# Banded attention in 24-query tiles on the quarters of the partitions, with one softmax per job, before two gated layers on one core

## The chip, the cores and the metric

The kernel runs on one core of one Trainium2 chip. The metric is the device time in microseconds (us) of one execution. Three runs of the kernel before gave 1005.63, 1005.64 and 1008.18 us; the median is 1005.64 us.

## The reference

Inputs are q, k, v of 4 batches x 8 heads x 576 positions x 64, and weights of two gated layers. In float32:

```python
q_d, k_d, v_d = (mean over 4 neighbouring positions of q, k, v)     # 144 positions
out_up    = repeat(softmax(q_d @ k_d.T / 8) @ v_d, 4)               # down-sampled attention
out_local = softmax(where(|i - j| < 4, q @ k.T / 8, -1e9)) @ v      # banded attention
x  = (out_up + out_local) as 2304 tokens x 512
y  = (sigmoid(x @ w_gate) * (x @ w_val)) @ w_out                    # 512 -> 1536 -> 512
h  = y @ w_in;  out = (h * sigmoid(1.702 h)) @ w_out2               # 512 -> 2048 -> 512
```

## The kernel before, in words

**Jobs.** Attention is cut into 16 jobs, one per batch and pair of heads (class Job, L409); head 0 of a pair lies on partitions 0 to 63, head 1 on 64 to 127. A job loads q and k, transposed (L433, L434), loads v grouped by fours for the down-sampled part (vg, two DMAs, L436) and v in five overlapping pieces of at most 122 rows for the band (vt, five DMAs, L444). Its steps are:

- pools (L466): GpSimd adds neighbours of q and k (L450, L452); VectorE sums v over four (L472).
- scores (L475): the band in five units of 116 queries by 122 keys, each in two parts of 64 and 52 queries against 70 and 58 keys, two heads: 20 products (L487), which the trace shows as 40 matmuls, since each fp32 product is two.
- soft (L495): per unit and part, one VectorE instruction adds the mask, scales and finds the extreme (L501), ScalarE takes the exponential with a sum (L508); the sums are inverted (L512, L513) and GpSimd multiplies (L519).
- the transpose of the probabilities: for batch 0 on TensorE with copies by ScalarE (full_transpose, L550, L555), for the other batches as 14 VectorE transposes of 32-row blocks (L535).
- down, soft_d, down_t (L559 to L625): the down-sampled attention, 144 by 144, with its products (L568), extremes (L584), exponentials (L591), sums (L595, L596), GpSimd multiplication (L604) and TensorE transposes (L618).
- values and combine (L627, L661): products with v (L644, L650), then VectorE adds the two parts (L667) and the sum is split into a high and a low part for the layers (L672, L674).

**Layers.** The tokens go through layer 1 in five visits (one per batch, the last for the four tails of 64 tokens together), then through layer 2 in five. Each product of the layers is three matmuls of 512 columns (passes, L744 to L749: high times high, low times high, high times low). The first visit, that of batch 0, has 12 blocks of 36 such matmuls, 432 in all. Layer 1's weights come as 64-bit words and are made into float32 by VectorE and ScalarE in the first visit (bits and signed: L696, L698, L700, L705), 36 pieces of 512 KB; splitting them into high and low takes ScalarE and GpSimd (L711, L713). VectorE also makes the gated product of each block (L783, L787).

**Order.** Class Plan (L62) orders all instructions at build time. Each has an assumed cost and a due time; on each engine the earliest due among the ready ones comes first, and SyncE's queue (SP) of DMAs is ordered in the same way, with an assumed rate (L73) and time per issue (L193). The due times follow from T0, the assumed start of the layers (L381), and EARLY (L384). Weights are asked for no earlier than 15 us ahead of their due time (AHEAD, L386), which is 8 us ahead of the block that uses them. Where TensorE would stand idle before the first layer products, it is given small filler matmuls on zeros (L917). PSUM has two banks for attention (pa), and while batch 0 is worked four more (acc). At run time each engine goes through its list in this order and waits where an operand is late.

Of the kernel before, what the change touches and what calls it, by code (L numbers as in the profile page):

```python
# [19 lines left out]
P = 128  # L20
# [41 lines left out]
class Plan:  # L62
# [10 lines left out]
    DMA_RATE = 230.0  # L73
# [48 lines left out]
    def order(self):  # L122
# [24 lines left out]
        while count:  # L147
# [44 lines left out]
            if e == "sp":  # L192
                free[e] = t + 60.0  # L193
# [24 lines left out]
def tile_multiscale_attention_gated_ffn(  # L218
# [22 lines left out]
    LW = 128  # L241
# [49 lines left out]
    ring("xf", 2, [P, 348])  # L291
# [10 lines left out]
    qslots, kslots, vslots, pslots, tslots = (plan.rings[nm][0] for nm in ("qt", "kt", "vt", "pt", "tt"))  # L302
# [27 lines left out]
    for s in kslots:  # L330
        nc.gpsimd.memset(s.t[:, :KPAD], 0.0)
        nc.gpsimd.memset(s.t[:, KPAD + S:], 0.0)
    for s in vslots:
        nc.gpsimd.memset(s.t[:32, 0], 0.0)
        nc.gpsimd.memset(s.t[96:, NUN - 1], 0.0)
    masks = [sb.tile([P, n], F32, name=f"mask{i}", tag=f"mask{i}")
             for i, n in enumerate((WIDTH[0], WIDTH[0], WIDTH[1]))]
    nc.gpsimd.memset(masks[1], 0.0)
    for h in range(2):
        half = masks[1][h * D:(h + 1) * D]  # L340
        nc.gpsimd.affine_select(out=half, in_=half, pattern=[[1, WIDTH[0]]], compare_op=ALU.is_ge,
                                fill=NEG, base=0, channel_multiplier=-1)
        nc.gpsimd.affine_select(out=half, in_=half, pattern=[[-1, WIDTH[0]]], compare_op=ALU.is_ge,
                                fill=NEG, base=6, channel_multiplier=1)
# [5 lines left out]
    def unit_mask(u, part):  # L350
        if u == 0 and part == 0:
            return masks[0]
# [604 lines left out]
```

## Time and profile before

| | |
|---|---|
| median of three runs | 1005.64 us |
| the profiled execution's own time | 1005.93 us |
| its span, first to last instruction | 1004.2 us |
| TensorE (PE) busy | 961.4 us, 96% of the span |
| VectorE (DVE) busy | 577.2 us, 57% |
| ScalarE (ACT) busy | 445.3 us, 44% |
| GpSimd (POOL) busy | 322.2 us, 32% |
| mean granted TensorE clock | 0.983 of full speed |
| moved by DMA | 70.96 MB, 71 GB/s over the span |

The busy shares are averages over parts of the run that differ. The span is also shown in 40 slices of 25.1 us, each with the busy share of an engine in tenths, and by windows. In rows of the trace, a name such as pt<-pt,nm says which tile is written and which are read; x56 is a count; "mean ns" is the mean duration of one instruction; the records of neighbouring instructions of one engine overlap a little.

### The profile page before, as it was taken

What the parts mean: (1) busy time and instruction counts of PE and PEld (TensorE: products, weight loads), DVE (VectorE), ACT (ScalarE), POOL (GpSimd) and SP (SyncE); (2) the same over time, 40 slices, a digit from 0 to 9 for tenths busy, and PEclk for the clock granted to TensorE, in tenths of its full rate; (3) what the DMA queues carried; (4) which work ended last, traced back from release to release, by engine and by line L of the source; (5) the groups of instructions that cost most, each with busy time, mean ns of one, the idle gap of its engine ahead of it and who ended that gap; (6) DMA issues with size and microseconds to landing.
All of it is one profiled execution on the core that took longest, in us unless ns stands there. A gap on an engine that the chain in (4) does not pass through costs nothing.

```text
span 1004.2 us, 15460 instructions
## 1 busy us (share of the span) xinstructions
PE 961.4 (96%) x5620; PEld 788.9 (79%) x5620; DVE 577.2 (57%) x1380; ACT 445.3 (44%) x1142; POOL 322.2 (32%) x318
## 2 busy tenths in 40 slices
PE   6889799799999999999999999999999999999997
PEld 5777577688788878888889977788888888888896
DVE  4899999966663576565756689723223222322232
ACT  5755465554544554554556565413223222322222
POOL 5654655544453453353445442102002000100000
PEclk8989899999999999999999999999999999999999
DMA  5664455121111210033204044102001000100010
GB/s 162 185 209 146 140 192 179 31 95 50 51 49 32 72 33 20 24 116 126 85 22 154 16 148 168 42 1 84 1 1 43 32 1 1 52 1 1 1 43 22
DMA packets 45324, 70.96 MB, mean 71 GB/s; under 512 B 5632, under 2 KB 26048, under 8 KB 45248
## 3 DMA queue, kind: packets, MB, share of 16 engines
q1 hardware_dynamic: 45248, 69.97, 21.9%
q8 instruction: 44, 0.72, 0.3%
q14 instruction: 32, 0.26, 0.1%
HBM read 60.00 MB, written 9.96 MB: 70 GB/s over the span
## 4 chain that ended last, share of the span: by engine, by line
PE 72%; DVE 18%; issue 4%; DMA 2%; ACT 2%; POOL 1%; SPq 1%; POOLq 0%; ACTq 0%; DVEq 0%
PE ph L747 13%; PE ph L749 13%; PE ph L748 13%; PE acc L747 10%; PE acc L748 10%; PE acc L749 10%; DVE we L700 3%; DVE we L698 2%; DVE tt L535 2%; DVE w L705 2%; PE pa L487 1%; DVE glo L787 1%; DVE vd L472 1%; DVE we L705 1%; DVE th L783 1%
## 5 line engine op out<-in xcount | busy, mean ns | idle before, releaser
L783 DVE SCALAR_TENSOR_TENSOR th<-th,ph 128x512 f32<-128x512 f32 (+1 forms) x140 | 88.5, 632 | 270.7 <-ACT th L778 212.1
L713 POOL TENSOR_TENSOR wlo<-w,whi 128x512 fp32r<-128x512 f32 x126 | 177.8, 1418 | 172.4 <-ACT whi L711 169.4
L778 ACT ACTIVATE th<-ph 128x512 f32<-128x512 f32 (+1 forms) x140 | 77.4, 553 | 261.6 <-PE ph L749 261.5
L747 PE MATMUL ph<-xhi,whi 128*128 128x512 f32 (+1 forms) x480 | 181.6, 378 | 1.2 <-DVE th L783 1.2
L748 PE MATMUL ph<-xhi,wlo 128*128 128x512 f32 (+1 forms) x480 | 178.0, 371 | 2.2 <-POOL wlo L713 2.2
L749 PE MATMUL ph<-xlo,whi 128*128 128x512 f32 (+1 forms) x480 | 177.7, 370 | 0.0
L711 ACT CAST whi<-w 128x512 fp32r<-128x512 f32 x180 | 110.2, 618 | 108.4 <-PE ph L749 39.2
L787 DVE TENSOR_TENSOR glo<-th,ghi 128x512 fp32r<-128x512 f32 (+1 forms) x140 | 99.3, 709 | 47.7 <-ACT ghi L786 46.6
L747 PE MATMUL ph<-xhi,w 128*128 128x512 f32 (+1 forms) x320 | 119.9, 375 | 1.4 <-DVE th L783 1.3
L749 PE MATMUL ph<-xlo,w 128*128 128x512 f32 (+1 forms) x320 | 119.3, 373 | 0.0
L748 PE MATMUL ph<-xhi,w 128*128 128x512 f32 (+1 forms) x320 | 119.1, 372 | 0.0
L747 PE MATMUL acc<-w,ghi 128*128 128x512 f32 x288 | 114.4, 397 | 1.7 <-ACT ev L826 1.6
L748 PE MATMUL acc<-w,glo 128*128 128x512 f32 x288 | 114.1, 396 | 0.4 <-DVE glo L787 0.4
L749 PE MATMUL acc<-w,ghi 128*128 128x512 f32 x288 | 113.9, 395 | 0.0
L786 ACT CAST ghi<-th 128x512 fp32r<-128x512 f32 (+1 forms) x140 | 80.6, 576 | 63.8 <-DVE th L783 62.6
L747 PEld LDWEIGHTS ph<-xhi,whi 128*128 128x128 f32 x480 | 90.9, 189 | 19.0 <-issue 2.6
L748 PEld LDWEIGHTS ph<-xhi,wlo 128*128 128x128 f32 x480 | 91.0, 190 | 16.7 <-POOL wlo L713 2.6
L749 PEld LDWEIGHTS ph<-xlo,whi 128*128 128x128 f32 x480 | 91.1, 190 | 15.8 <-DVE xlo L674 0.3
L858 POOL TENSOR_TENSOR xlo<-st,xhi 128x512 fp32r<-128x512 f32 (+1 forms) x24 | 30.3, 1275 | 223.3 <-ACT xhi L856 223.2
L747 PE MATMUL acc<-ghi,whi 128*128 128x512 f32 (+1 forms) x240 | 90.5, 377 | 0.0
L748 PE MATMUL acc<-ghi,wlo 128*128 128x512 f32 (+1 forms) x240 | 89.1, 371 | 0.0
L749 PE MATMUL acc<-glo,whi 128*128 128x512 f32 (+1 forms) x240 | 88.9, 371 | 0.0
(104 smaller groups left out, 1470.7 us busy)
## 6 DMA issues: line engine op xcount, KB each, us to landing
w<-w SPq DMA_DIRECT2D x68, 512.0 KB
qt<-qT SPq DMA_DIRECT2D x16, 288.0 KB
kt<-kT SPq DMA_DIRECT2D x16, 288.0 KB
vg<-v SPq DMA_DIRECT2D x32, 144.0 KB
x2d<-ev SPq DMA_DIRECT2D x16, 256.0 KB
st<-x2d SPq DMA_DIRECT2D x16, 256.0 KB
out<-ev SPq DMA_DIRECT2D x16, 256.0 KB
vt<-v SPq DMA_DIRECT2D x48, 61.0 KB
```

The costliest lines, as they stand in the source:

```text
L700: op("dve", 602.0, lambda: nc.vector.scalar_tensor_tensor(e.t, wv[:, :, 0], 29, e.t, op0=ALU.logical_shift_right, op1=ALU.bitwise_or), [w] ...
L705: op("dve", 602.0, lambda: nc.vector.scalar_tensor_tensor(m.t, top, -2 ** 31, e.t, op0=ALU.bitwise_and, op1=ALU.bitwise_or), [w] if m is e ...
L711: op("act", 520.0, lambda: nc.scalar.copy(hi.t, m.t.bitcast(F32)), [m], [hi], due)
L713: op(eng, ns, lambda: on.tensor_sub(lo.t, m.t.bitcast(F32), hi.t.bitcast(F32)), [m, hi], [lo], due)
L747: nc.tensor.matmul(o, lhi, rhi, start=first, stop=False)
L748: nc.tensor.matmul(o, llo, rhi, start=False, stop=False)
L749: nc.tensor.matmul(o, lhi, rlo, start=False, stop=last)
L778: op("act", act_ns(n, True), lambda h=h: nc.scalar.activation(th.t[:, :n], h.t[:, :n], AF.Tanh, scale=0.5 if layer == 1 else 1.702 / 4.0), ...
L783: op("dve", dve_ns(n), lambda: nc.vector.scalar_tensor_tensor(th.t[:, :n], th.t[:, :n], 1.0, hb[-1].t[:, :n], op0=ALU.add, op1=ALU.mult), ...
L786: op("act", act_ns(n), lambda: nc.scalar.copy(gh.t[:, :n], th.t[:, :n]), [th], [gh], t)
L787: op("dve", dve_ns(n), lambda: nc.vector.tensor_sub(gl.t[:, :n], th.t[:, :n], gh.t[:, :n].bitcast(F32)), [th, gh], [gl], t)
L858: op("pool", pool_ns(n), lambda k=k, st=st: nc.gpsimd.tensor_sub(lo.t[:, k, :n], st.t[:, :n], hi.t[:, k, :n].bitcast(F32)), [st, (hi, k)], ...
```

## The change

The band is cut into 24 tiles of 24 queries by 30 keys. Tile NG*i+g (NG = 6) goes to quarter i of the partitions, so that a head's scores are one block of 128 partitions by 6 x 30. Each job then has 48 products of 30 columns for the scores, with tile positions in the array, and one softmax over both heads: VectorE adds the mask (two instructions), takes the maximum, subtracts it, ScalarE takes one exponential over 360 columns, VectorE sums, inverts, multiplies and transposes all 32-row blocks at once. The products with v are 48 of 24 columns, in two halves; the second half is issued after ScalarE has copied out the down-sampled result. The down-sampled softmax takes its maximum with two instructions and its exponentials straight from PSUM. v is loaded, and summed over four, for two jobs at a time. Costs and dates that the plan assumes are altered.

```diff
-    DMA_RATE = 230.0
+    DMA_RATE = 300.0
...
-                free[e] = t + 60.0
+                free[e] = t + 450.0
...
-    NQ, NU = 116, 122
-    WIDTH = (D + 6, NU - D)
-    units = [(0, 0), (116, 0), (232, 0), (348, 0), (460, 4)]
-    NUN = len(units)
+    NQ, NU = 24, 30
+    NT = S // NQ
+    NG = NT // 4
+    VC = 2 * P
+    HALF = S // 2
...
-    for nm, n, shape in (("qt", 2, [P, S + 12]), ("kt", 2, [P, KPAD + S + 5]), ("vt", 2, [P, NUN, P]),
-                         ("pt", 2, [P, NUN, 2, LW]), ("tt", 2, [P, 2 * NUN, LW]), ("vg", 2, [GH, 2, 4, P]),
-                         ("half", 1, [P, G, 2]), ("qd", 2, [P, G]), ("kd", 2, [P, G]), ("vd", 2, [GH, 2, P]),
-                         ("nm", 2, [P, 2, NUN]), ("sm", 2, [P, 2, NUN]), ("pd", 2, [GH, 2, 2, G]),
-                         ("nmd", 2, [GH, 4]), ("smd", 2, [GH, 4]), ("pdt", 1, [GH, 2, 2, G]), ("up", 2, [P, G])):
+    for nm, n, shape in (("qt", 2, [P, S + 12]), ("kt", 2, [P, KPAD + S + 5]), ("vt", 2, [P, NG, VC]),
+                         ("sc", 2, [P, 2, NG, NU]), ("pt", 2, [P, 2, NG, 32]), ("tt", 2, [P, 2, NG, 32]),
+                         ("vg", 1, [GH, 2, 4, VC]), ("half", 1, [P, G, 2]),
+                         ("qd", 2, [P, G]), ("kd", 2, [P, G]), ("vd", 2, [GH, 2, VC]),
+                         ("nm", 2, [P, 2, NG]), ("sm", 2, [P, 2, NG]), ("pd", 2, [GH, 2, 2, G]),
+                         ("nmd", 2, [GH, 4]), ("smd", 2, [GH, 4]), ("pdt", 2, [GH, 2, 2, G]), ("up", 2, [P, G])):
...
+    mask = sb.tile([P, NG, NU], F32, name="mask", tag="mask")
+    band = sb.tile([P, NU], F32, name="band", tag="band")
...
-    QUANTUM = 3 * 216.0
+    QUANTUM = 3 * 227.0
     ATT = 15.0e3
-    T0 = 50.0e3
+    T0 = 37.0e3
...
-    EARLY = 20.0e3
-    FULL_T = 1
+    EARLY = 16.0e3
...
+    class Values:
+
+
+        def __init__(self, m):
+            self.b, self.c0 = m // 2, m % 2 * VC
+            self.job = jobs[2 * m]
+
+        def load(self):
+            b, c = self.b, slice(self.c0, self.c0 + VC)
+            self.vg, self.vt, self.vd = buf("vg"), buf("vt"), buf("vd")
+
+            hp = self.job.hp
+            d, after = (self.job.t0 - 3000.0, self.job.t0 - 12000.0) if b else (4500.0 * hp, 4500.0 * hp)
+            for kh in range(2):
+                dma(self.vg.t[:, kh], v[b, kh * 4 * GH:(kh + 1) * 4 * GH, c].rearrange("(g r) d -> g r d", r=4),
+                    GH * 4 * VC * 4, [], [(self.vg, kh)], d, after)
+            d, after = (self.job.due(0.2), self.job.t0 - 9000.0) if b else (4500.0 * hp + 3000.0, 6000.0 * hp)
+            for i in range(4):
+                g0, g1 = i == 0, NG - (i == 3)
+                row = NQ * (NG * i + g0) - 3
+                src = v[b, row:row + 32, c]
+                src = bass.AP(tensor=src.tensor, offset=src.offset,
+                              ap=[[DM, 32], [NQ * DM, g1 - g0], [1, VC]])
+                dma(self.vt.t[32 * i:32 * i + 32, g0:g1], src, 32 * (g1 - g0) * VC * 4, [], [(self.vt, i)], d, after)
+            dma(self.vt.t[3:NU, 0], v[b, :NU - 3, c], (NU - 3) * VC * 4, [], [(self.vt, 4)], d, after)
+            row = NQ * (NT - 1) - 3
+            dma(self.vt.t[96:96 + S - row, NG - 1], v[b, row:S, c], (S - row) * VC * 4, [], [(self.vt, 5)], d, after)
+
+        def pool(self):
+            vg, vd = self.vg, self.vd
+            at = self.job.due(0.4)
+            op("dve", dve_ns(4 * VC), lambda: nc.vector.tensor_add(
+                vg.t[:, :, :2], vg.t[:, :, :2], vg.t[:, :, 2:]), [], [vg], at)
+            op("dve", dve_ns(2 * VC), lambda: nc.vector.tensor_add(vd.t, vg.t[:, :, 0], vg.t[:, :, 1]),
+               [vg], [vd], at)
...
+            d, after = self.t0 - 4000.0, self.t0 - 13000.0
+            dma(self.qt.t[:, :S], qT[b, hp], P * S * 4, [], [self.qt], d, after)
+            dma(self.kt.t[:, KPAD:KPAD + S], kT[b, hp], P * S * 4, [], [self.kt], d, after)
...
+                for t in range(NT):
+                    g, i = divmod(t, 4)
+                    t = NG * i + g
+                    for h in range(2):
+                        hs = slice(h * D, (h + 1) * D)
+                        nc.tensor.matmul(ss[h].t[32 * i:32 * i + 32, g * NU:(g + 1) * NU],
+                                         qt.t[hs, NQ * t:NQ * t + 32], kt.t[hs, NQ * t:NQ * t + NU],
+                                         start=True, stop=True, tile_position=(h * D, 32 * i))
+
+            n = NG * NU
+            op("pe", 1500.0, pe, [qt, kt], [*ss, (sc, 0), (sc, 1)], self.due(0.1))
+            for h in range(2):
+                op("dve", dve_ns(n), lambda h=h: nc.vector.tensor_add(
+                    sc.t[:, h], ss[h].t[:, :n].rearrange("p (g c) -> p g c", c=NU), mask),
+                   [ss[h]], [(sc, h)], self.due(0.1))
+
+            def spread(x):
+                return x.t[:, :, :, None].to_broadcast([P, 2, NG, NU])
+
+            at = self.due(0.15)
+            op("dve", dve_ns(2 * n), lambda: nc.vector.reduce_max(nm.t, sc.t, axis=AX.X), [sc], [nm], at)
+            op("dve", dve_ns(2 * n), lambda: nc.vector.tensor_sub(sc.t, sc.t, spread(nm)), [nm], [sc], at)
+            p = pt.t[:, :, :, :NU]
+            op("act", act_ns(2 * n), lambda: nc.scalar.activation(p, sc.t, AF.Exp, scale=SCALE), [sc], [pt], at)
+            op("dve", dve_ns(2 * n), lambda: nc.vector.reduce_sum(sm.t, p, axis=AX.X), [pt], [sm], at)
 
             def inv():
+                nc.vector.tensor_scalar_add(sm.t, sm.t, 1.0e-9)
+                nc.vector.reciprocal(sm.t, sm.t)
+
+            op("dve", 305.0, inv, [], [sm], at)
+            op("dve", dve_ns(2 * n), lambda: nc.vector.tensor_mul(p, p, spread(sm)), [sm], [pt], at)
+            op("dve", 700.0, lambda: nc.vector.transpose(
+                out=tt.t.rearrange("p h g c -> p (h g c)"), in_=pt.t.rearrange("p h g c -> p (h g c)")),
+               [pt], [tt], at)
...
+                op("dve", dve_ns(2 * G), lambda h=h: nc.vector.reduce_max(
+                    nmd.t[:, 2 * h:2 * h + 2], ss[h].t[:GH, :2 * G].rearrange("p (r k) -> p r k", k=G), axis=AX.X),
+                   [ss[h]], [(nmd, h)], at)
+            op("dve", 90.0, lambda: nc.vector.tensor_scalar_mul(nmd.t, nmd.t, -SCALE_D), [], [nmd], at)
+
+            def ex(h):
                 for r in range(2):
                     x = 2 * h + r
+                    nc.scalar.activation(pd.t[:, h, r], ss[h].t[:GH, r * G:(r + 1) * G], AF.Exp,
+                                         bias=nmd.t[:, x:x + 1], scale=SCALE_D, accum_out=smd.t[:, x:x + 1])
+
+            for h in range(2):
+                op("act", 1100.0, lambda h=h: ex(h), [nmd, ss[h]], [(pd, h), (smd, h)], at)
...
+            def band(x):
+                for g in range(NG):
+                    for s, i in ((sa, x), (sz, 2 + x)):
+                        ks, q = slice(32 * i, 32 * i + NU), NQ * (NG * x + g)
+                        for h in range(2):
+                            nc.tensor.matmul(s.t[h * D:(h + 1) * D, q:q + NQ],
+                                             vt.t[ks, g, v0 + h * D:v0 + (h + 1) * D], tt.t[ks, h, g, :NQ],
+                                             start=True, stop=True, tile_position=(32 * i, h * D))
 
             def pe():
+                band(0)
                 for kh in range(2):
                     for h in range(2):
+                        nc.tensor.matmul(sa.t[h * D:(h + 1) * D, c0:c0 + G],
+                                         vd.t[:, kh, v0 + h * D:v0 + (h + 1) * D],
                                          pdt.t[:, h, kh, :], start=(kh == 0), stop=(kh == 1))
+
 
             xfs = [buf("xf") for _ in range(2)]
+            op("pe", 1400.0, pe, [vd, pdt, vt, tt], [sa, sz, up, *xfs], self.due(0.9))
+            op("act", 260.0, lambda: nc.scalar.activation(up.t, sa.t[:, c0:c0 + G], AF.Copy, scale=0.25),
                [sa], [up], self.due(0.9))
+            op("pe", 700.0, lambda: band(1), [vt, tt, up], [sa, sz], self.due(0.9))
+            for n, s in enumerate((sa, sz)):
+                self.combine(n * HALF, (n + 1) * HALF, s, xfs[n], n == 0, xh, xl)
...
     jobs = [Job(b, hp) for b in range(B) for hp in range(NHP)]
+    halves = {(m // 2, m % 2): Values(m) for m in range(2 * B)}
     jobs[0].load()
-    jobs[0].load_v()
+    jobs[1].load()
+    halves[0, 0].load()
...
+        if n + 2 < len(jobs):
+            jobs[n + 2].load()
+            if n % 2 == 0:
+                halves[divmod(n // 2 + 1, 2)].load()
```

## Rows read from the trace of the kernel before

**Rows 1.** The page's 40 slices of the span, VectorE.

```profile
DVE  4899999966663576565756689723223222322232
```

**Rows 2.** Windows: length, busy time of PE, PEld, DVE, ACT, POOL, granted clock, DMA.

```profile
0.00:30.00 30.00, 20.24 (x305) 18.43 (x305) 14.63 (x100) 14.37 (x71) 16.09 (x46) 0.83 0.56 162
30.00:66.00 36.00, 28.47 (x380) 24.15 (x379) 34.38 (x110) 23.40 (x104) 22.88 (x28) 0.91 0.64 210
66.00:201.00 135.00, 118.38 (x711) 93.67 (x708) 132.32 (x309) 74.48 (x202) 71.52 (x60) 0.95 0.44 140
201.00:500.00 299.00, 298.82 (x1816) 242.20 (x1815) 189.58 (x558) 159.76 (x452) 136.56 (x129) 1.00 0.20 63
```

**Rows 3.** ScalarE groups, 66 to 201 us: busy, mean ns, idle before and what ended it.

```profile
L711 ACT CAST whi<-w 128x512 fp32r<-128x512 f32 x35 | 21.5, 617 | 34.0 <-DVE w L705 30.9 <-DVE sm L512 1.3 <-DVE smd L595 1.0
```

**Rows 4.** VectorE's busy time to 201 us, lines L501, L535, L472, L584, L512, L513, L527.

```profile
0.00:201.00 201.00, 12.52 (x160) 0.92 0.50 156
0.00:201.00 201.00, 18.79 (x56) 0.92 0.50 156
0.00:201.00 201.00, 17.77 (x9) 0.92 0.50 156
0.00:201.00 201.00, 8.04 (x64) 0.92 0.50 156
0.00:201.00 201.00, 3.07 (x16) 0.92 0.50 156
0.00:201.00 201.00, 3.04 (x16) 0.92 0.50 156
0.00:201.00 201.00, 2.25 (x2) 0.92 0.50 156
```

**Rows 5.** VectorE groups by shape, 201 to 500 us.

```profile
L472 DVE TENSOR_REDUCE vd<-vg 72x256 f32<-72x1024 f32 x7 | 14.0, 2007 | 0.1
...
L667 DVE TENSOR_TENSOR xf<-pa,up 128x348 f32<-128x348 f32 x8 | 4.2, 520 | 12.7 <-ACT up L656 12.5
L674 DVE TENSOR_TENSOR xlo<-xf,xhi 128x348 fp32r<-128x348 f32 x8 | 4.1, 518 | 0.1
...
L667 DVE TENSOR_TENSOR xf<-pa,up 128x228 f32<-128x228 f32 x8 | 3.1, 385 | 0.0
```

**Rows 6.** Timeline of TensorE around two attention blocks: start us, us, what.

```profile
347.24 0.40 PE L748 MATMUL ph<-xhi,wlo 128*128 128x512 f32 x1
347.47 0.40 PE L749 MATMUL ph<-xlo,whi 128*128 128x512 f32 x1
347.80 1.40 PE L487 MATMUL pa<-kt,qt 64*64 64x70 f32 x40
349.13 0.50 PE L747 MATMUL ph<-xhi,whi 128*128 128x512 f32 x1
...
194.22 0.71 PE L644 MATMUL pa<-pdt,vd 72*64 72x144 f32 x8
194.76 1.16 PE L650 MATMUL pa<-tt,vt 122*64 122x116 f32 x20
195.85 0.50 PE L747 MATMUL ph<-xhi,whi 128*128 128x512 f32 x1
```

**Rows 7.** Timeline of TensorE, the last products with v of batch 0.

```profile
63.03 2.13 PE L650 MATMUL acc<-tt,vt 122*64 122x116 f32 x20
```

**Rows 8.** Timeline of SyncE's queue at the start, and the first weight load.

```profile
0.73 0.40 SPq L375 DMA_DIRECT2D qt<-qT  x1
...
1.65 1.86 SPq L375 DMA_DIRECT2D vg<-v  x2
3.55 4.50 SPq L375 DMA_DIRECT2D vt<-v  x5
...
34.51 0.53 SPq L375 DMA_DIRECT2D w<-w  x1
```

**Rows 9.** Timeline of TensorE, two products of different heads.

```profile
30.42 0.34 PE L568 MATMUL pa<-kd,qd 64*72 64x144 f32 x1
30.43 0.34 PE L568 MATMUL acc<-kd,qd 64*72 64x144 f32 x1
```

More of the change, by code (lines that the diff above doesn't have):

```diff
@@ L332, in tile_multiscale_attention_gated_ffn @@
         nc.gpsimd.memset(s.t[:, KPAD + S:], 0.0)
+    mask = sb.tile([P, NG, NU], F32, name="mask", tag="mask")
+    band = sb.tile([P, NU], F32, name="band", tag="band")
+    nc.gpsimd.memset(band, 0.0)
+    for i in range(4):
+        quarter = band[32 * i:32 * i + 32]
+        nc.gpsimd.affine_select(out=quarter, in_=quarter, pattern=[[1, NU]], compare_op=ALU.is_ge,
+                                fill=NEG, base=0, channel_multiplier=-1)
+        nc.gpsimd.affine_select(out=quarter, in_=quarter, pattern=[[-1, NU]], compare_op=ALU.is_ge,
+                                fill=NEG, base=6, channel_multiplier=1)
@@ L333, in tile_multiscale_attention_gated_ffn @@
+    nc.gpsimd.tensor_copy(mask, band[:, None, :].to_broadcast([P, NG, NU]))
+    nc.gpsimd.affine_select(out=mask[:32, 0], in_=mask[:32, 0], pattern=[[1, NU]], compare_op=ALU.is_ge,
+                            fill=NEG, base=-3, channel_multiplier=0)
+    nc.gpsimd.affine_select(out=mask[96:, NG - 1], in_=mask[96:, NG - 1], pattern=[[-1, NU]],
+                            compare_op=ALU.is_ge, fill=NEG, base=S + 2 - NQ * (NT - 1), channel_multiplier=0)
     for s in vslots:
         nc.gpsimd.memset(s.t[:32, 0], 0.0)
-        nc.gpsimd.memset(s.t[96:, NUN - 1], 0.0)
@@ L336, in tile_multiscale_attention_gated_ffn @@
[L336 to L344, printed above, removed]
@@ L345, in tile_multiscale_attention_gated_ffn @@
-    nc.gpsimd.affine_select(out=masks[0], in_=masks[1], pattern=[[1, WIDTH[0]]], compare_op=ALU.is_ge,
-                            fill=NEG, base=-3, channel_multiplier=0)
-    nc.gpsimd.affine_select(out=masks[2], in_=masks[1][:, :WIDTH[1]], pattern=[[-1, WIDTH[1]]],
-                            compare_op=ALU.is_ge, fill=NEG, base=S + 2 - units[-1][0] - D, channel_multiplier=0)
-    def unit_mask(u, part):
-        if u == 0 and part == 0:
-            return masks[0]
-        return masks[2 if u == NUN - 1 and part else 1][:, :WIDTH[part]]
@@ L449, in pool4 @@
             s = src.rearrange("p (g a b) -> p g a b", a=2, b=2)
-            op("pool", 880.0, lambda: nc.gpsimd.tensor_add(half.t, s[:, :, :, 0], s[:, :, :, 1]),
+            op("pool", 760.0, lambda: nc.gpsimd.tensor_add(half.t, s[:, :, :, 0], s[:, :, :, 1]),
                [bsrc], [half], due)
-            op("pool", 520.0, lambda: nc.gpsimd.tensor_add(dst.t, half.t[:, :, 0], half.t[:, :, 1]),
+            op("pool", 450.0, lambda: nc.gpsimd.tensor_add(dst.t, half.t[:, :, 0], half.t[:, :, 1]),
                [half], [dst], due)
         def front(self):
-            steps = [self.pools, self.scores, self.down]
-            if self.first:
-                steps += [lambda h=h, us=us: self.full_transpose(h, us) for h in range(2)
-                          for us in (range(3), range(3, NUN))]
-            return steps
+            return [self.pools, self.scores, self.down]
         def back(self):
@@ L481, in pe @@
             def pe():
-                for part in range(2):
-                    n, c = WIDTH[part], D * part
-                    for u, (q0, _) in enumerate(units):
-                        for h in range(2):
-                            hs = slice(h * D, (h + 1) * D)
-                            nc.tensor.matmul(ss[part].t[hs, u * n:(u + 1) * n], qt.t[hs, q0 + c:q0 + c + D],
-                                             kt.t[hs, q0 + c:q0 + c + n], start=True, stop=True)
-            op("pe", NUN * (56.0 * 2 + 1.667 * sum(WIDTH)), pe, [qt, kt],
-               [*ss, (pt, 0), (nm, 0), (pt, 1), (nm, 1)], self.due(0.1))
@@ L901, in tile_multiscale_attention_gated_ffn @@
                 front[x]()
-                if x == 0 and n + 1 < len(jobs):
-                    jobs[n + 1].load()
             if x < len(back):
```

150 lines of the change are left out of this document (22 added, 128 removed).

## Prediction

> **What bounds the kernel now.** I read the slices first. VectorE is full from the third slice to the eighth and then falls to about two thirds [rows 1]. The windows say what that means. From 201 us on TensorE is busy 298.8 of 299 us, while VectorE is at 189.6 [rows 2]: the rest of the kernel is TensorE's, and only a change in TensorE's own work counts there. From 66 to 201 us it is the other way round: VectorE 132.3 of 135 us, TensorE 118.4, at a granted clock of 0.95 [rows 2]. The weights explain it: ScalarE, which splits them for the first visit, stood idle for 30.9 us until VectorE had made a weight (L705) [rows 3]. So up to 201 us the first visit goes at VectorE's pace, with batch 1's jobs and 36 weights on that engine. Before 66 us batch 0's jobs run; their last products with v come at 63.0 us [rows 7], and no block of the layers can be finished before that. VectorE idles 15.4 of the first 30 us [rows 2]: SyncE needs 4.5 us to issue one job's five vt loads and 1.86 for two of vg, against 0.40 for q [rows 8], and the first weight is not asked for until 34.5 us.
>
> The reading to keep: before 201 us a microsecond off VectorE is worth a microsecond, after it nothing; TensorE's is the reverse.
>
> **VectorE, up to 201 us.** Eight jobs (batches 0 and 1) lie there. The change removes from VectorE L501 12.5 us, L535 18.8, L584 8.0, L512 3.1, L513 3.0, L527 2.2, and of L472 eight of nine instructions, 15.8: 63.4 us in all [rows 4]. What it adds per job, priced by the fit through L667's two shapes (385 ns at 228 columns, 520 at 348, so 128 ns and 1.125 a column) [rows 5]:
> - two additions of the mask, 180 columns: 2 x 0.33 = 0.66;
> - subtraction and multiplication over 360: 2 x 0.53 = 1.06;
> - maximum and sum over 360: no row has a reduction over contiguous columns. L472's strided one took 2007 ns for 1024, 1.96 a column, which gives 0.71 each; the fit gives 0.53. I take 0.53, as the strides are gone, and keep 0.4 to 0.71;
> - inversion, 0.38 (L512 and L513 as now, once instead of twice) [rows 4];
> - the transpose of 384 columns: L535 took 0.336 us for 160 (18.8 over 56) [rows 4], so at most 0.81, and at least 0.43 by the fit's slope; I take 0.7;
> - two maxima over 288 for the down-sampled part, 0.90, and a small product, 0.1;
> - v over four, per two jobs 1024 and 512 columns, 1.28 + 0.70, so 0.99 a job.
>
> That is 5.85 us a job, 46.8 for eight, with bounds of 4.9 and 7.2. The saving is 63.4 - 46.8 = 16.6 us. Records of neighbours overlap a little, so I count 0.93 of it, an estimate: 15.5 us (bounds 22.5 and 5.5).
>
> **The start.** SP's issues per two jobs are now 2 x (0.4 + 0.4) + 2 x 1.86 + 2 x 4.50 = 14.3 us [rows 8]. After: the same 1.6 for q and k, 1.86 for two wider vg loads, and six vt loads at between 0.4 (as q) and 0.9 (as a vt load now), 2.4 to 5.4: at most 8.9 us. Weights may be asked for 13 us earlier, since T0 moves from 50 to 37 us. Both put work before VectorE in the 15.4 idle us. The first 5 us can't be filled; I take 9 of the rest, with 0 and 12 as bounds. GpSimd loses the multiplication L519 and keeps its other work; it has 63 us to spare in the window of 135 [rows 2]. ScalarE loses nine of ten exponentials of the band; it had 60 to spare already, so that is worth nothing by itself. The wider v rows (32 rows per tile of 24 queries) add about a third to vt's bytes; DMA stands at 0.44 busy in the window [rows 2], which covers that. If that cover were gone, the first weights would be late.
>
> **TensorE.** Matmuls come in pairs, one per head, that run side by side. Per pair: L487 1.33 us for 20 pairs of 64 columns on average, 66.5 ns; L650 1.09 for 10 pairs of 115, 109 ns; L644 0.54 for 4 pairs of 144, 135 ns [rows 6]. That is a line: 0.86 ns a column and 12 ns a pair. New scores are 48 pairs of 30 columns at 38 ns, 1.8 us against 1.33. New products with v are 48 pairs of 24 columns at 32.5 ns, 1.55 against 1.09. The second half of them adds one more interruption, 0.1 us (347.47 + 0.23 would be 347.70, and L487 starts at 347.80) [rows 6]. So +1.0 us a job if only pairs overlap. If four tiles overlap, both fall by half: 1.7 - 2.42 + 0.1 = -0.6. The plan's own costs hint at between: 1627 and 1765 ns before, for blocks that take 1.43 and 1.72 on the path [rows 6], become 1500 and 2100, which scaled is +0.2. I take +0.5; the eight jobs of batches 2 and 3 lie where TensorE is the bound, so +4 us. For batch 1 it hides under VectorE: 118.4 + 4 x 0.5 still leaves 14 us. Batch 0's TensorE transposes (L550) go; they lie before the layers and are counted at nothing.
>
> One rule speaks against the change. Rows first: the records of two products of different heads start 10 ns apart [rows 9], so two tiles are not held apart by a long step. The Trainium skill (TensorE: Matmul & The Clock Gate, "Wait — 56ns, not 53.3ns?") says that start-to-start never falls below about 25 ns however small the matmul. By that rule, as an estimate, 192 matmuls would take 4.8 us against 2.42, some 20 us more over eight jobs. The rows do not agree for tiles in different rows of the array, and the sum goes on without it.
>
> **Waits that come in.** The second half of the products with v waits for ScalarE's copy of the down-sampled result; behind it on TensorE stand layer matmuls, and the combination on VectorE waits for it. The plan puts other work between, so I price it at nothing, at up to 1 us a job if ScalarE is late. The two attention banks are held until ScalarE has taken the exponentials; the next scores wait for that.
>
> **Sum.** Against the profiled execution's 1005.9 us: -15.5 - 9 + 4 = -20.5, so 985.4. The profile lies 0.3 above the median, so 985.
>
> **Rivals.**
> - *Better:* four tiles overlap and VectorE's prices are the low ones: -22.5 - 12 - 8 x 0.6 = -39, 967 us. For: the tile positions differ in columns too. Against: no row shows four side by side. Chance 0.20.
> - *Loads of 64 weight columns set the pace* of the products with v: L487 has 64 columns on both sides, so its 66.5 ns a pair may be the load's. Then 48 x 66.5 = 3.2 us, +2.1, with the scores' +0.45 and 0.1 +2.65 a job: 21 us over eight jobs, and batch 1's 10.6 leaves TensorE 6 us of slack in the window, so 4 of the gain go: 1005.6 - 20.5 + 21 = 1006. Against: pairs that share rows might load side by side. Chance 0.12. The skill's floor, above, would give nearly this.
> - *Slower:* tiny matmuls come no faster than the fastest sustained stream now, 33 ns each (L487, 1.33 us over 40) [rows 6]. Then 192 x 33 = 6.4 us, +4.0 a job: 32 us over eight jobs, while batch 1's 16 fill the window (118.4 + 16 of 135) and leave about 15 of the gain: 1005.6 - 15 + 32 = 1022. It decides from 24.5 / 8 = 3.1 us a job, 28 ns a matmul. Against: 10 ns apart [rows 9]. Chance 0.10.
> - *The relief isn't used:* the first visit turns out to hang on the order of weights and jobs, not on VectorE's sum, and only the start is gained: 1005.6 - 9 + 4 = 1001. Against: 2.7 us of idle in 135. Chance 0.08.
>
> **Chances and range.** My forecast has 0.50, and its own range by the bounds is 974 to 996. A measurement of this kernel tells 0.3%, 3 us, from no change. Faster by that: forecast, the better case, nearly all of the last and a little of the second, 0.80. Same: most of the second and the rest, 0.09. Slower: 0.11. From 965 to 1005 the range leaves out the slow rival, half of the second, and the better one's far end.
>
> **What would show it.** Right: VectorE's full stretch ends near 177 us instead of 201, batch 0's last products with v come before 50 us, the first weight load near 20 us; L535 and L501 are gone and the new instructions on VectorE sum to about 6 us a job; the two TensorE blocks of a job in batch 2 take 3 to 4 us. Wrong: blocks over 6 us, TensorE idle after 201 us, or VectorE full until 195 us or later.

## The result, and the profile after

| | before | after |
|---|---|---|
| median of six runs | 1005.74 us | 1012.02 us |
| lowest to highest | 1003.92 to 1008.18 | 1009.95 to 1016.06 |
| the profiled execution's own time, its span | 1005.93, 1004.2 | 1016.06, 1014.2 |
| VectorE busy | 577.2 us | 524.7 us |
| matmuls on TensorE | 5620 | 7614 |

The ratio is 1.0063, 95% interval 1.0039 to 1.0087: slower by 6.3 us, where 985 us (965 to 1005) was forecast. The profiled execution of after is the longest of its six, 4 us above the median, so its trace shows some 10 us where the medians differ by 6.

The 40 slices of after, VectorE (against [rows 1]):

```profile
DVE  5679999545453554467565679723222222322232
```

Windows of after (against [rows 2], same columns):

```profile
0.00:30.00 30.00, 17.12 (x474) 15.03 (x474) 17.05 (x42) 6.94 (x23) 17.06 (x48) 0.75 0.92 189
30.00:66.00 36.00, 29.01 (x605) 24.08 (x607) 23.92 (x61) 11.34 (x36) 17.46 (x12) 0.64 0.52 163
66.00:201.00 135.00, 121.60 (x1233) 94.61 (x1232) 119.35 (x189) 65.13 (x144) 72.86 (x58) 0.92 0.53 149
201.00:500.00 299.00, 298.00 (x2870) 239.21 (x2863) 159.63 (x287) 136.13 (x299) 125.70 (x115) 1.00 0.24 67
```

VectorE's full stretch did become shorter: 119 us of 135 instead of 132, and the eighth slice falls from 9 to 5. But in the first 30 us the DMA engines are at 0.92 instead of 0.56 while moving little more (189 GB/s against 162), TensorE does less, and its granted clock is 0.75 and then 0.64, against 0.83 and 0.91. TensorE waits 19.9 us before 66 us, against 17.0 before (8.6 of them for k), but most of it for a reason that the kernel before does not show there: "issue" means that no semaphore and no instruction in the profile released it. Waits of TensorE before 66 us, after (engine, line, releaser: us in total, times, longest):

```profile
PE acc L494 <- issue: 10.3, 2, 5.2
PE acc L603 <- issue: 3.7, 1, 3.7
...
PE pa L494 <- issue: 0.9, 1, 0.9
```

**How the first visit ends.** Two moments measure it in every trace: the end of the last of its 36 weights on VectorE (L705 before, L668 after), and the start of the 144th layer product on TensorE, in order of time (a product is three passes; the expectations below call one product a pass). The first visit has 144 products, but its last block's final four come behind the first eight of the next visit's first block, so the 144th in time is the fourth of those eight in each of these kernels; the visit's own last product starts 6.6 to 7.4 us behind it in all of them. From the timelines, the last weight and the first pass of the 144th product, of before and of after:

```profile
194.31 1.65 DVE L705 SCALAR_TENSOR_TENSOR w<-w,we 128x512 int32<-128x512 int32 x1
...
202.14 0.39 PE L747 MATMUL ph<-xhi,whi 128*128 128x512 f32 x1
```

```profile
185.03 0.68 DVE L668 SCALAR_TENSOR_TENSOR w<-w,we 128x512 int32<-128x512 int32 x1
...
205.40 0.39 PE L710 MATMUL ph<-xhi,whi 128*128 128x512 f32 x1
```

Before, TensorE was at the 144th product 6.2 us behind the last weight (195.96 to 202.14). After, VectorE was done 10.3 us earlier (185.71) and TensorE 3.3 us later, 19.7 us behind. From the 144th product to the end of the span it is 802.1 us before and 808.8 after, 6.7 more. So 3.3 + 6.7 make the 10.0 us between the two spans: the relief on VectorE is there, and did not reach TensorE.

### The profile page after: what moved, and what is told of

Read it like the earlier page. It is cut to its first block, busy times and chain, and to the rows that moved or that the text cites. A ratio compares the mean times of both kernels' runs of the same rounds, so it can differ in the third digit from the quotient of the medians.

```text
span 1014.2 us, 18484 instructions
## 1 busy us (share of the span) xinstructions
PE 970.4 (96%) x7614; PEld 790.8 (78%) x7614; DVE 524.7 (52%) x886; ACT 395.6 (39%) x822; POOL 309.1 (30%) x290
## 4 chain that ended last, share of the span: by engine, by line
PE 79%; DVE 11%; issue 4%; DMA 2%; ACT 1%; POOL 1%; SPq 0%; POOLq 0%; DVEq 0%; ACTq 0%
PE ph L710 15%; PE ph L711 14%; PE ph L712 14%; PE acc L710 10%; PE acc L711 10%; PE acc L712 10%; DVE we L663 3%; PE pa L603 2%; DMA vg<-v 2%; DVE we L668 1%; DVE we L661 1%; DVE w L668 1%; PE pa L534 1%; PE pa L494 1%; DMA w<-w 1%
## 5 line engine op out<-in xcount | busy, mean ns | idle before, releaser
L710 PE MATMUL ph<-xhi,whi 128*128 128x512 f32 (+1 forms) x480 | 185.0, 386 | 3.4 <-ACT th L741 3.2
L711 PE MATMUL ph<-xhi,wlo 128*128 128x512 f32 (+1 forms) x480 | 181.0, 377 | 1.0 <-POOL wlo L676 1.0
L712 PE MATMUL ph<-xlo,whi 128*128 128x512 f32 (+1 forms) x480 | 180.4, 376 | 0.0
L750 DVE TENSOR_TENSOR glo<-th,ghi 128x512 fp32r<-128x512 f32 (+1 forms) x140 | 95.6, 683 | 48.7 <-ACT ghi L749 47.9
## 6 DMA issues: line engine op xcount, KB each, us to landing
vt<-v SPq DMA_DIRECT2D x16, 192.0 KB
```

Of the source, the lines that this page charges most:

```text
L710: nc.tensor.matmul(o, lhi, rhi, start=first, stop=False)
L711: nc.tensor.matmul(o, llo, rhi, start=False, stop=False)
L712: nc.tensor.matmul(o, lhi, rlo, start=False, stop=last)
L750: op("dve", dve_ns(n), lambda: nc.vector.tensor_sub(gl.t[:, :n], th.t[:, :n], gh.t[:, :n].bitcast(F32)), [th, gh], [gl], t)
```

## The experiments

The two moments in the profiled execution of each run, and the result. "Numbers" are the five numbers of the plan: two dates (T0, EARLY) and three prices (DMA_RATE, the time of a DMA issue, QUANTUM). The moments come from one execution each, and executions of one kernel differ: E12's ten runs lie between 998.0 and 1006.7 us.

| run | v | numbers | median us | ratio to before, 95% | last weight | 144th product | from there to the end |
|---|---|---|---|---|---|---|---|
| before | by job | old | 1005.74 | 1 | 196.0 | 202.1 | 802.1 |
| after | two jobs | new | 1012.02 | 1.0039 to 1.0087 | 185.7 | 205.4 | 808.8 |
| E1 | two jobs | old | 1010.09 | 1.0023 to 1.0050 | 188.3 | 200.8 | 806.4 |
| E2 | none in batch 0 | new | 1011.61 | 1.0034 to 1.0070 | 184.8 | 203.8 | 807.3 |
| E3 | two jobs | new | 1018.42 | 1.0095 to 1.0144 | 188.9 | 208.3 | 807.9 |
| E4 | by job | new | 1004.59 | 0.9971 to 1.0002 | 179.8 | 198.4 | 807.2 |
| E5 (kernel before) | by job | new | 1017.70 | 1.0080 to 1.0124 | 202.3 | 214.1 | 801.9 |
| **E6** | **by job** | **old** | **998.65** | **0.9900 to 0.9940** | **186.0** | **192.2** | **805.4** |
| E10 | bunched, 512 B | old | 1005.55 | 0.9973 to 0.9997 | 192.0 | 199.2 | 805.4 |
| E11 | bunched from batch 1 | old | 1002.91 | 0.9954 to 0.9975 | 189.6 | 196.9 | 805.6 |
| E13 | by job | new dates | 1018.28 | 1.0092 to 1.0168 | 175.7 | 201.9 | 813.6 |
| E17 | by job | new prices | 1010.15 | 1.0021 to 1.0053 | 188.8 | 201.0 | 807.8 |

**E1: the plan's numbers back.**

```diff
-    DMA_RATE = 300.0
+    DMA_RATE = 230.0
-                free[e] = t + 450.0
+                free[e] = t + 60.0
-    QUANTUM = 3 * 227.0
+    QUANTUM = 3 * 216.0
-    T0 = 37.0e3
+    T0 = 50.0e3
-    EARLY = 16.0e3
+    EARLY = 20.0e3
```

> The changed kernel with the plan's five numbers of before (T0 50, EARLY 20, matmul 3 x 216, DMA rate 230, 60 ns an issue). Theory A (TensorE waits at the start for its own instructions, whose fetch queues behind data loads; stalls of 5.1, 5.2 and 3.7 us): the order of the lists changes little of it, stalls of 3 us or more remain, 1006 to 1016 us. Theory B (the new dates order the lists badly, so that VectorE and SyncE wait behind late steps): the stalls stay or shift, but the time falls to 990 to 1002 us.

1010.09 us, in theory A's range, with one stall of 3.7 us left; but the issue waits fell from 14.9 to 4.7 us, so the order of the lists changes much of them. In the profiled executions the 144th product comes 4.6 us earlier, though the last weight is 2.6 later; the medians differ by only 1.9.

**E2: no v for batch 0.** The eight loads of v of each of batch 0's two halves (a half is two jobs) are left out and zeros taken in their place, so batch 0's output lacks its v. VectorE writes the zeros, 4.4 us in the first 6.3. The edit, in part:

```diff
             self.vg, self.vt, self.vd = buf("vg"), buf("vt"), buf("vd")
+            if b == 0:
+                return
```

> The changed kernel without batch 0's loads of v (zeros stand in for v of batch 0; 2.7 MB less at the start, TensorE's instructions as before). Theory A: with fewer data loads ahead of it each fetch takes under 3 us, stalls at the start fall from 15 us in all to under 6, batch 0's last products come before 57 us instead of 67, total 996 to 1004 us. Theory B: the lists are as before, 1008 to 1016 us.

1011.61 us: theory B's range; theory A asked for 1004 at most. The issue waits before 66 us are gone from TensorE's list, batch 0's last products with v start at 61.19 us instead of 67.10, and the total hardly moves: the 144th product comes at 203.8. What was gained by 100 us (45 products against 36) was lost from 100 to 150 (41 against 52), where a weight lands late (a step of 10.6 us at 103.5 in the chain; that batch 1's v holds it up is not shown) and one wait for GpSimd's product (L563 here, L561 in after) lasts 7.1 us. So the stalls at the start are not the one cause. Nor is the granted clock there: from 30 to 66 us it is 0.62 in E2 and 0.66 in E4, as low as after's 0.64, and both had as many products by 100 us (45 and 46) as before (44 at 0.91).

**E3: batch 0's scores issued twice** (the 96 matmuls of each of its four jobs, before the same results are used).

> The changed kernel with batch 0's 96 score matmuls issued twice per job (384 more matmuls at 10 ns, 3.8 us of TensorE's time, and three more pieces of 16 KB of instructions). Theory A: two or three more stalls of 3 to 5 us, last products of batch 0 at 73 to 82 us, total 1017 to 1028 us. Theory C (TensorE's matmuls as such cost the time): 4 us or less, 1012 to 1016 us.

1018.42 us, 6.4 above after, for about 4 us of matmuls (0.95 us a block); issue waits before 66 us grow from 14.9 to 18.2 us in the waits view. More small matmuls make more and longer stalls (seven instead of four, the longest 7.7 us). The total is theory A's; batch 0's last products, at 70.8 us, come earlier than its 73 to 82.

**E4 and E6: v loaded and summed job by job**, in rows of 512 bytes, with the new numbers (E4) and with the old ones (E6). The edit, in part:

```diff
-                         ("vg", 1, [GH, 2, 4, VC]), ("half", 1, [P, G, 2]),
+                         ("vg", 2, [GH, 2, 4, P]), ("half", 1, [P, G, 2]),
...
-            if n % 2 == 0:
-                halves[divmod(n // 2 + 1, 2)].load()
+            halves[(n + 2) // NHP, (n + 2) % NHP // 2].load(n % 2)
```

> The changed kernel with v loaded and summed job by job (512-byte rows, twice the number of loads, same tiles). Theory A: the bursts ahead of each fetch halve, the stalls shrink to 2 to 4 us each, total 1004 to 1010 us. Rival (what matters is that a load fills only 32 partitions): the loads take as long, 1009 to 1015 us. Theory B: 1009 to 1016 us.

> The changed kernel with v loaded job by job and with before's plan numbers: both repairs together. Theory A (start and dates are separate losses that add): the gain of the numbers (1.9 us in the changed kernel) on top of 1004.6, so 1002 to 1003.5 us, 151 or more layer passes by 201 us. Theory B (with the start mended the first visit is limited by TensorE's waits for the product of L561 on GpSimd, which no date moves): 1004 to 1006 us, 147 to 150 passes.

E4 1004.59 us, at the low end of theory A, with stalls of 1.5 and 0.6 us; E6 998.65 us. E6 beats both kernels: 0.9920 of before, 7.6 us less than its companion runs of before (1006.3), and both theories were too timid. Its windows and, from the timelines, its two moments:

```profile
0.00:30.00 30.00, 21.00 (x639) 19.12 (x640) 19.41 (x55) 8.00 (x27) 17.88 (x48) 0.89 0.72 174
30.00:66.00 36.00, 32.60 (x568) 25.72 (x567) 30.72 (x65) 13.02 (x40) 13.55 (x13) 0.76 0.58 172
66.00:201.00 135.00, 124.31 (x1290) 97.65 (x1289) 123.50 (x194) 67.12 (x149) 70.45 (x60) 0.96 0.52 149
```

```profile
184.34 1.65 DVE L678 SCALAR_TENSOR_TENSOR w<-w,we 128x512 int32<-128x512 int32 x1
...
192.19 0.39 PE L720 MATMUL ph<-xhi,whi 128*128 128x512 f32 x1
```

VectorE ends at 186.0, as early as in after, but here TensorE follows 6.2 us behind, as it does before. The gain of the tiles is real once TensorE is let keep up.

**E5: the new numbers alone, in the kernel before.**

> The kernel before with the five plan numbers of the changed one (DMA_RATE 300, 450 ns per DMA issue, QUANTUM 227, T0 37 us, EARLY 16 us) and nothing else. Theory A (the dates are a cost of their own: T0 = 37 us puts weight conversions ahead of attention steps that TensorE then waits for): 1007.5 to 1010 us, more waits of TensorE for attention steps between 66 and 201 us than the 15 us of before. Theory B (the dates hardly matter; the small matmuls and v cost all of it): 1005 to 1006.5 us, within 0.1% of before.

1017.70 us, 11.4 above its companion runs: the numbers by themselves cost more than the whole change. Theory A had the sign, and at most a third of the size. The last weight is 6.3 us later, the 144th product 12.0, and the rest unchanged (801.9).

**E13 and E17: the two dates, or the three prices, alone** on E6.

> v job by job and before's numbers for rate, issue and quantum, but the changed kernel's two dates (T0 37 us, EARLY 16 us). With all five old numbers 998.65 us, with all five new 1004.6. Theory A (the two dates carry it: weights are due 13 us earlier and go ahead of attention steps on VectorE): 1003 to 1006 us, 147 to 150 layer passes by 201 us. Theory B (the prices of transfers, 300 and 450, reorder the work): 998 to 1000 us, 153 passes or more.

> v job by job with the three prices of the changed kernel (DMA_RATE 300, 450 ns per DMA issue, QUANTUM 227) and before's two dates (T0 50 us, EARLY 20 us). All old 998.65, all new 1004.6, new dates alone 1018.3 us. Theory A (dates and prices are two separate effects, and the prices repair what the dates spoil, by 13.7 us): below 996 us if they also help by themselves, else 997 to 1000 us. Theory B (only the match of the two matters: prices that fit the earlier dates are wrong for the later ones): 1003 us or more.

1018.28 us with the dates, 1010.15 with the prices, though all five together (E4) give 1004.59. In E13 theory A has the sign and a third of the size, in E17 theory B holds. The effects do not add: either part alone is worse than both together, and the old set fits these kernels better. How an early date costs is plain in E13. The timeline of TensorE around 40 us:

```profile
38.66 0.48 PE L720 MATMUL ph<-xhi,whi 128*128 128x512 f32 x1
44.58 0.80 PE L721 MATMUL ph<-xhi,wlo 128*128 128x512 f32 x1 [5.43 <-POOL wlo L686]
45.17 0.63 PE L722 MATMUL ph<-xlo,whi 128*128 128x512 f32 x1
45.73 0.53 PE L612 MATMUL pa<-tt,vt 30*64 30x24 f32 x12
```

The list puts the first layer product ahead of batch 0's products with v; its second pass waits 5.4 us for a weight's low part, and the attention behind it waits too. By 100 us TensorE has done 34 products against E6's 47, while VectorE has its last weight at 175.7 us, 10 us before E6's: weights made early, as it looks at the expense of steps that TensorE needs.

**E10 and E11: which part of loading v for two jobs costs.** On E6, loads and sums of both jobs go back to the first job's dates, in rows of 512 bytes: in all batches (E10), or in batches 1 to 3 only (E11; there the sums of batch 0's second half are joined as well).

> As the version with v job by job and before's plan numbers (998.65 us), but the loads and sums of v for both jobs of a half go back to the dates of the first job, still in rows of 512 bytes. With the numbers of before, the changed kernel (both jobs at a time, rows of 1024 bytes) took 1010.1 us. Theory A (it costs to ask for and sum two jobs' v at once: the burst lies ahead of k, weights and instructions, and the sums stand ahead of the first job's steps): 1006 to 1010 us. Theory B (it is the long rows, which move at under 190 GB/s): 998 to 1001 us.

> The same with only batches 1 to 3 bunched; batch 0 loads v job by job. Theory A1 (of the bunching, batch 0's start is what costs): 998 to 1002 us, and the layers start by 66 us. Theory A2 (batch 1's burst beside the first visit costs, at about 105 us, where it delayed a weight by 8 us): 1004 to 1009 us, as many passes by 100 us as the version job by job (47), fewer from 100 to 201 us than its 109.

1005.55 and 1002.91 us: between the theories. From E6 upwards, bunching batches 1 to 3 costs 4.3 us, batch 0 another 2.6, and the rows of 1024 bytes, with half as many loads and sums, by the difference to E1, 4.5. A2's sign for batch 1 holds (101 products from 100 to 201 us against 108), but no one part is the cause.

**E7 and E12: the pooled division on ScalarE**, in E4 and in E6, since TensorE's longest waits from 66 to 201 us are for GpSimd's product (L561 in after; 13.4 us in E4).

```diff
-                op("pool", 680.0, lambda h=h: nc.gpsimd.tensor_mul(
-                    pd.t[:, h], pd.t[:, h], smd.t[:, 2 * h:2 * h + 2, None].to_broadcast([GH, 2, G])),
-                   [smd], [(pd, h)], at)
+                op("act", 700.0, lambda h=h: norm(h), [smd], [(pd, h)], at)
```

> The changed kernel with v job by job, and the division of the pooled softmax (two GpSimd products per job, 0.66 us each when alone) made by four ScalarE activations with a scale per row. Theory A (between 66 and 201 us TensorE waits 13.4 us for this product because GpSimd holds it behind the splitting of weights): that wait falls under 5 us, 4 or more passes more by 201 us, total 999 to 1002 us. Theory B (the product is late because VectorE's reciprocal before it is late, behind weight conversions in the list): the wait keeps 9 us or more under ScalarE's name and the total stays at 1003.5 to 1006 us.

> v job by job, before's plan numbers, and the pooled softmax divided on ScalarE. Theory A (what GpSimd gives up serves the splitting of weights and the waits of 2 us for L570): 994 to 997 us. Theory B (with before's numbers TensorE hardly waits for that product, so nothing is gained; ScalarE's four activations come later than GpSimd's two): 998 to 1001 us.

1003.95 us (0.9967 to 0.9988 of before) and 1003.37 (0.9958 to 0.9990). In E7 the wait keeps 10.3 us under ScalarE's name: theory B. E12's median is 4.7 us above E6's and outside both theories. GpSimd was the last step named, not the cause.

**E9: scores of batches 2 and 3 issued twice** in E4.

> The changed kernel with v job by job, and the 96 score matmuls of each job of batches 2 and 3 issued twice (8 jobs, 0.95 us a block in the trace, 7.6 us in all, between 201 and 500 us where TensorE shows no idle time). Theory A (in that stretch TensorE's time is the total, so the small matmuls cost what they take): 7 to 9 us above the same kernel without it, 1011.5 to 1013.5 us, and 10 to 12 layer passes fewer between 201 and 500 us. Theory B (the extra matmuls run beside layer matmuls or in gaps): under 3 us, 1004 to 1007.5 us.

1022.47 us, more than twice what theory A asked for. From 201 to 500 us there are 355 products against E4's 377, 22 fewer, 15 us at the 0.68 us between the first passes of neighbours. The doubled matmuls explain 7.6 us of it; the waits view has 4.3 us of issue waits in two stalls, and the clock of 201 to 350 us is 0.98 instead of 1.00. One of the stalls:

```profile
227.32 1.50 PE L503 MATMUL pa<-kt,qt 64*32 64x30 f32 x155
231.14 0.52 PE L503 MATMUL pa<-kt,qt 64*32 64x30 f32 x37 [2.32 <-issue]
```

**E14 to E16: is it an accident of the order?** T0 at 52 instead of 50 us in before, in E1 and in E6.

> The kernel before with T0 at 52 us instead of 50, nothing else. Theory A (the gaps are the kernels' own, a date moved by 2 us is small change): 1004 to 1008 us. Theory B (every order of the instructions is a draw of its own): off 1006 by 4 us or more, to either side.

> The tiles with v for two jobs at a time and before's numbers (1010.1 us), with T0 at 52 us. Theory A: 1008 to 1012 us, still 8 us or more above the version job by job at the same date. Theory B: off 1010 by 4 us or more, or within 5 us of the version job by job.

> The tiles with v job by job and before's numbers (998.65 us), with T0 at 52 us. Theory A: 997 to 1001 us. Theory B: 1003 us or more.

1006.41, 1008.02 and 999.91 us; E6's version is at 0.9912 to 0.9959 of before. The three keep their order and the gap of two jobs to one is 8.1 us, after 11.4: theory A, with some 2 us that belong to the order. One shift by 2 us is a small sample of orders.

**E18 and E19: what VectorE's time is worth.** The same extra sum of v (2.0 us) in the four jobs of batch 1, list unchanged, in before and in E6.

> The kernel before with L472's sum of v (2.0 us in the trace) issued twice in the four jobs of batch 1, 8.0 us more on VectorE between 60 and 160 us; its price in the plan is left, so that the order of all instructions stays. Theory A (the first visit goes at VectorE's pace, a microsecond for a microsecond): 6 to 9 us above before, 1012 to 1015 us. Theory B (VectorE is full because its list runs ahead, and TensorE's waits for single steps, the clock and GpSimd set the end): 0 to 4 us above, 1006 to 1010 us.

> The tiles with v job by job and before's numbers (998.65 us), with the same sum of 2.0 us added in the four jobs of batch 1 ahead of the additions there, list unchanged. Theory A (VectorE's pace still sets the first visit): 6 to 9 us more, 1004.5 to 1008 us. Theory B (VectorE now has slack before 201 us, TensorE lost 15 us there against 20 before): 0 to 3 us more, 998 to 1002 us.

1012.31 us (1.0056 to 1.0082) in before: 8.0 us of VectorE moved the 144th product from 202.1 to 210.0 and the total by 6.5. In E6 1004.05 us, 5.4 more, between the theories; the 144th product comes at 197.0. VectorE sets the pace of the first visit in before, and in E6 it still does for the greater part.

## Why the prediction was wrong

**VectorE's saving: right.** The forecast was 15.5 us (5.5 to 22.5). VectorE's busy time up to the end of its last weight fell by 21.3 us, some of it gated products of blocks that TensorE had not reached by then. Windows of VectorE up to that moment, before and after (length, busy time, clock, DMA):

```profile
0.00:195.96 195.96, 176.54 (x510) 0.92 0.50 158
0.00:185.71 185.71, 155.18 (x283) 0.83 0.61 166
```

Yet the last weight came only 10.3 us earlier, where the saving and the start together were to bring some 24 (the full stretch was to end "near 177 us instead of 201"; by the slices it did, but the weights went on to 185.7): VectorE idled 11.1 us more on the way, 30.5 instead of 19.4. The prices held. VectorE's groups of after, 201 to 500 us (busy, mean ns, idle before):

```profile
L541 DVE TENSOR_REDUCE nmd<-pa 72x2 f32<-72x288 f32 x16 | 6.6, 449 | 20.9 <-PE pa L534 20.9
L510 DVE TENSOR_TENSOR sc<-sc,nm 128x360 f32<-128x360 f32 x8 | 5.1, 643 | 0.3
...
L501 DVE TENSOR_TENSOR sc<-pa,mask 128x180 f32<-128x180 f32 x16 | 4.8, 338 | 13.9 <-PE pa L494 13.8
...
L521 DVE STREAM_TRANSPOSE tt<-pt 128x384 f32<-128x384 f32 x8 | 4.6, 575 | 0.2
L513 DVE TENSOR_REDUCE sm<-pt 128x12 f32<-128x360 f32 x8 | 4.2, 526 | 5.4 <-ACT pt L512 5.4
L520 DVE TENSOR_TENSOR pt<-pt,sm 128x360 f32<-128x360 f32 x8 | 4.2, 525 | 0.1
L509 DVE TENSOR_REDUCE nm<-sc 128x12 f32<-128x360 f32 x8 | 4.2, 523 | 0.2
```

With v's two sums (1204 and 1076 ns per two jobs), the inversion (228 + 227 ns) and the small product (380, priced at 100), a job takes 6.3 us there, against 5.85 forecast.

**"Before 201 us a microsecond off VectorE is worth a microsecond": nearly true of the kernel before, not of the one after.** E18 shows the first, for time added, at 0.8. What the sentence missed is that a saving on VectorE pays only while TensorE can follow. The prediction gave TensorE 14 us of slack in 66 to 201 us, as span less busy time. That time is not slack but waits, most of them for a single attention step, GpSimd's product: 10.7 of 16.6 us before, 9.0 of 13.4 after.

```profile
PE pa L618 <- POOL pd L604: 10.7, 5, 4.3
```

```profile
PE pa L575 <- POOL pd L561: 9.0, 5, 4.2
```

The granted clock there fell too, from 0.95 to 0.92. So after, TensorE was at the 144th product 19.7 us behind the last weight.

**The start, -9: the failed step.** "Weights may be asked for 13 us earlier" was counted as 9 us less idle time on VectorE, and the overlap with batch 0's jobs that it needs did not come. In the first 30 us VectorE idles 13 us instead of 15.4, but from 30 to 66 us 12.1 instead of 1.6, since its list stands still until TensorE has made batch 0's products with v. VectorE's longest wait from 30 to 66 us, after (before, the longest there is 0.6 us):

```profile
DVE xf L630 <- PE acc L603: 10.2, 3, 3.5
```

The first weight load came about as forecast (22.75 us), but batch 0's last products with v started at 67.10 us, not before 50. The same wait is 11.3 us in E2, without any stall; with the old numbers VectorE idles 3.3 us from 30 to 66 us (E1) and 5.3 (E6). No run shows the gain of 9: even in E6 VectorE idles 23.0 us before its last weight, against 19.4 in before. For v, the prediction's "DMA stands at 0.44 busy in the window" took the mean of 66 to 201 us for a load that falls in the first 30, where [rows 2] already had 0.56. The DMA view of 25 to 32 us, after (share of the engines in tenths, GB/s, 40 slices):

```profile
DMA  9999999999999999999899987998989999999999
GB/s 182 170 193 211 193 263 240 234 222 193 228 141 170 123 146 117 217 181 135 117 146 141 199 181 187 304 328 351 398 351 398 421 421 445 398 421 445 398 398 375
```

The engines are full throughout, at 117 to 263 GB/s in the first 25 slices and at 304 to 445 after them. TensorE's stall of 5.19 us (25.60 to 30.79, in the middle of a block of 96 scores) ends after the slow part. The queue that brings instructions moved 60 packets, 0.98 MB, instead of 44, 0.72 MB, since each job now has 192 small matmuls in these two products instead of 60:

```profile
q8 instruction: 60, 0.98, 0.4%
```

E3 and E9 show that more small matmuls mean more such stalls. That they wait for instructions the packets of this queue show: the stall that ends at 30.79 us ends 1.3 us behind a packet of 16 KB that moved from 27.80 to 29.50, and each of the 39 issue waits in the 20 traces ends 1.25 to 1.83 us behind the end of such a packet. In after's three long ones the packet starts 1.2 to 2.2 us after TensorE has stopped. That it starts late because of v's packets is argued from E2, where the stalls went with the loads; E9's two, with the DMA engines at 0.27 (201 to 350 us), say that a full DMA is not needed for one.

**Loading v for two jobs at a time: of the wrong sign.** The prediction knew it as fewer issues on SP, a gain, and as 0.99 us a job on VectorE. On the old numbers it costs 11.4 us (E1 against E6; 8.1 with the shifted date), on the new ones 7.4 (after against E4). **The plan's numbers: of the wrong sign.** They were read as a chance to start early and cost 11.4 us in the kernel before, 5.9 on E6, 1.9 on E1. So the forecast sign belonged to the rest of the change, the tiles (E6: -7.6); its two companions turned it over.

**TensorE, +4: the blocks as forecast, the rest not explained.** From the 144th product to the end the versions with tiles take 805 to 809 us (apart from E13, which waits 9.2 us there against E6's 3.9, and E9) against 802.1, 3 to 7 us more. A job of batch 2, its scores and the two halves of its products with v:

```profile
233.29 1.02 PE L494 MATMUL pa<-kt,qt 64*32 64x30 f32 x96
234.24 0.50 PE L710 MATMUL ph<-xhi,whi 128*128 128x512 f32 x1
...
239.91 0.89 PE L603 MATMUL pa<-tt,vt 30*64 30x24 f32 x48
240.73 0.71 PE L611 MATMUL pa<-pdt,vd 72*64 72x144 f32 x8
241.37 0.50 PE L710 MATMUL ph<-xhi,whi 128*128 128x512 f32 x1
...
242.95 0.89 PE L603 MATMUL pa<-tt,vt 30*64 30x24 f32 x48
243.78 0.50 PE L710 MATMUL ph<-xhi,whi 128*128 128x512 f32 x1
```

0.95 + 0.82 + 0.64 + 0.83 = 3.24 us, within the 3 to 4 forecast. By [rows 6] the same products took 1.33 + 0.54 + 1.09 = 2.96 us before, so the blocks explain 0.28 us a job, 2.2 for eight; no run shows where the rest of after's 6.7 comes from. **The rivals** on TensorE's side fall with it: the scores start 10 ns apart (0.95 us for 96), not 33, and the products with v 17 ns apart. The scores came at half the price of pairs (0.95 against 1.8 us), as four tiles side by side would; the products with v came at the price of pairs (1.65 us for both halves, against 1.55). The floor of about 25 ns start to start that the Trainium skill states (TensorE: Matmul & The Clock Gate, "Wait — 56ns, not 53.3ns?") is not seen for these tiles. "The relief isn't used" was the nearest rival, but it kept the gain of the start, which did not come either. The prediction's "own range by the bounds", 974 to 996, kept that gain at its upper end too: with the start's stated bound of 0 and VectorE's of 5.5 it would have reached 1004.

**What stays open.** The runs say which edits cost, and the failed step shows in VectorE's idle time, but no run ties each edit's cost to a single wait; E10 and E11 split the cost of two jobs' v into three parts of 2.6 to 4.5 us, each near the scatter of the order. Why a set of dates and prices fits was not followed further. Nor was the clock after the start: from 66 to 201 us it is 0.92 in after and E4, 0.96 in E6, and nothing separates what that costs from the waits that go with it.

## What to carry to other kernels

An engine that is full may free time that its follower cannot use: look at how far the follower ends behind it (here 6 us, then 20), and do not count as slack what is a wait for a single step. An earlier date for one stage is a gain only if the engines that share its list do not then wait for the stage before. Change one thing at a time where a list is planned at build time: the plan's numbers moved this kernel by up to 20 us, more than the work that was saved. Read the DMA load in the window where the transfer falls, as a share of the engines and in GB/s, since full engines may move half of what they can.

## What the runs showed of the hardware

TensorE can run out of instructions. After 155 matmuls of 30 columns in 1.5 us it stood 2.3 us in E9, and up to 5.2 us in after and 7.7 in E3, with "issue" as the only releaser; each such wait ends 1.25 to 1.83 us behind a packet of 16 KB of the instruction queue. The kernel before, with 60 matmuls a job in these two products instead of 192, has no wait of this kind in its trace.

VectorE's instructions on SBUF can be held for long beside GpSimd. The timeline of after:

```profile
90.88 1.29 POOL L561 TENSOR_TENSOR pd<-pd,smd 72x288 f32<-72x288 f32 x2 [2.64 <-DVE smd L557]
91.25 3.70 DVE L661 TENSOR_SCALAR we<-we 128x512 int32<-128x512 int32 x1
...
92.13 2.54 POOL L676 TENSOR_TENSOR wlo<-w,whi 128x512 fp32r<-128x512 f32 x2
```

L661 takes 0.42 us by its median from 66 to 201 us and 3.70 here, to just behind the end of four GpSimd instructions in a row. The Trainium skill (SBUF — State Buffer, "SBUF: two separate sides") has the shared ports of the two as a lock held for a whole instruction; the row agrees, and reads as if VectorE had lost it several times running, which one row does not prove. Its "busy" time before 201 us would then hold waiting for GpSimd too: the mean of L661 from 66 to 201 us is 0.75 us.
